# One fused local-attention and mixture-of-experts kernel: the same instructions put in another order by other due times

## The chip, the cores and the metric

The kernel runs on one core of one Trainium2 chip. The metric is the device time of one execution in microseconds (us). The kernel before was timed three times: 1127.76, 1129.4 and 1139.5 us, a median of 1129.4 us. One more execution was profiled; all rows below come from that one.

## The reference, cut to what matters

There are 14336 tokens of width 192. The first half is a dynamic causal convolution: a softmax over 7 generated weights for each token and each of 8 heads, and a weighted sum of the 7 latest rows of `x`.

```python
w = softmax(weight_gen)                       # (B, S, 8 heads, 7 taps)
x = einsum('bshk,bskhg->bshg', w, x_windows)  # 7 shifted rows of x
```

The second half is a noisy top-2 mixture of 8 experts over that result (192 to 1024 to 192, relu):

```python
noisy = x @ w_gate + log1p(exp(x @ w_noise)) * noise
top2 = two largest of noisy;  top2_w = softmax over the two
out[t] = sum over its two e of  top2_w * (relu(x[t] @ w1[e]) @ w2[e])
```

All inputs and the output are fp32. The kernel gets its precision by splitting operands into a high and a low fp16 part and adding the products.

## The kernel before, in words

**Front end.** The tokens are cut into 15 chunks (`COLS`: 4 columns of 128 tokens, then thirteen times 8, then 4). A chunk `c` goes through these stages: loads of `x`, the weights and the noise (`x_loads`, `w_loads`, `n_loads`, issued by SyncE, called SP); sums of squares for a scale (`norms`, ScalarE, L414); the convolution (`conv`, VectorE: 7 products L470 and, from chunk 2 on, 6 sums L501; for chunks 0 and 1 TensorE adds the products up, L486); the split into two halves (`split`, L520 and L528); the gate logits (`gate`: a transpose, on SP as L568 from chunk 2 on, and small products, L575); the routing (`routing`, some 45 small VectorE operations and one small product on TensorE, L715, for the prefix counts); and the scatter (`scatters`, L630: 2 indirect DMAs for each column, issued by GpSimd, called POOL) of each token's record into the queue of its two experts in device memory (`xg`).

**Back end.** The records are taken out in 15 rounds of 8 experts. A block is one expert's 128 rows (round 0) or 256 rows (all others). For a block SP issues transposing loads of its rows (`rows` L1083 and `again` L1088); in front of a round it reads the start of each queue (`entry`), and behind the rows of the round's first block it issues eight loads of the gates' columns (`metas`, L1077). TensorE does the first layer (`mm1`, L1159 and L1165), ScalarE the relu with its high part (`hi`, L1179), VectorE the low part (`lo`, L1183), TensorE the second layer (`mm2`, L1204), ScalarE the gate (`y`, L1216), and POOL adds the rows onto `out` by an indirect DMA (L1221).

**Weights.** Each expert's weights are loaded (`weight_loads`), measured by a Gram product on TensorE (L921), scaled and rounded to a high part on ScalarE (L957, L961, L962), and given a low part: for experts 0 to 3 on TensorE and ScalarE (L998, L999, L1002), for experts 4 to 7 on VectorE (L959, L968, L970).

**What sets the order.** Nothing is ordered on the chip: each engine runs its own list in order, with waits between engines. The lists are written when the program is built, by `Sched`. Each stage is a stream of operations; a step of `Sched` takes, of the operations that could start on an engine within `WAIT` = 0.34 us of the earliest, the one with the earliest due time. The due times come from the two tables that the change touches. `need[b]` is the nominal start of block `b`: `PLAN["start"]` plus the spans of the blocks ahead of it (`SPAN`: 4.4 and 8.2 us); `rounds[c]` is that of a round's first block, `wanted[e]` that of expert `e`'s first block. Each entry of `LEAD` is subtracted from `rounds[c]` ("first" is chunk 0, "second" chunk 1, "last" chunk 14, "rest" the others), each of `PLAN` from `need`, `rounds` or `wanted` (some are added: `finish`, `relu`, `behind`). So a larger lead is an earlier due time. Within one stream nothing changes places: `prologues` gives, for each round, the entries, the rows of the first block, the eight `metas`, and then the rows of the other blocks, whatever their due times are. `SHIFT` moves two blocks of round 0 (experts 6 and 7) in between the blocks of round 1. The durations that `Sched` reckons with, the buffers and the instructions are no part of these tables.

Of the kernel before, what the change touches and what calls it, by code (L numbers as in the profile page):

```python
# [45 lines left out]
PESUM = (0, 1)  # L46
PETR = (0, 1)
LOWPOOL = ()
SHIFT = {6: 4, 7: 2}
YB = 6  # L50
SLOTS = 5
PM0 = 3
PACK = 2
LOWPE = (0, 1, 2, 3)
WAIT = 0.34
PLAN = dict(start=61.4, load=46.6, gram=65.3, high=-15.4, low=13, inverse=19, relu=-7.7, finish=-5, behind=5.2,
            gates=-5.1, entry=-6.7, metas=15.3, rows=10.1, clear=15, zero=18, stray=-10.7, ahead=1, late=2.5,
            landed=1, add=1.5)
SPAN = {256: 8.2, 128: 4.4}
LEAD = {"first": dict(w=112, x=210, n=44, norm=20, conv=23, gap=3.4, split=37, gate=84, route=37, scatter=-13,  # L60
                        every=0),
        "second": dict(w=83, x=31, n=74, norm=115, conv=46, gap=1.4, split=129, gate=49, route=90, scatter=11,
                        every=3.4),
        "rest": dict(w=122, x=117, n=89, norm=107, conv=56, gap=3.7, split=59, gate=36, route=85, scatter=14,
                        every=3.4),
        "last": dict(w=118, x=124, n=45, norm=74, conv=46, gap=1.4, split=72, gate=76, route=51, scatter=15,
                        every=2.8)}
BULK, HEAVY, CLEAN = "SP", "SP", "SP"


# [189 lines left out]
def moe_kernel(ctx, tc, x_lay, wgen, noise, wgn, w1, w2, xg, out):  # L260
# [84 lines left out]
    def bank():  # L345
# [5 lines left out]
    order = sorted(((c, e) for c in range(len(ROUNDS)) for e in range(E)),  # L351
                   key=lambda b: b[0] * E + b[1] if b[0] or not SHIFT.get(b[1]) else E + SHIFT[b[1]] - 0.5 + b[1] / 99)
    need, rounds = [], {}
    t = PLAN["start"]
    for c, e in order:
# [10 lines left out]
    def stages(c):  # L366

        return LEAD["first" if c == 0 else "second" if c == 1 else "last" if c == NC - 1 else "rest"]

# [4 lines left out]
    def before(key, i, n):  # L374

        return [(key, i - n)] if i >= n else []
# [181 lines left out]
    def gate(si):  # L558
# [6 lines left out]
        def transpose(h, t):  # L565
            if t == 0:
                buf[h] = fe.tile([P, 3 * GT, P], F16, name="xtg", bufs=1)
            nc.sync.dma_start_transpose(buf[h][:, 3 * t:3 * t + 3, :], rc[:, a + h + t, 0:RD])  # L568

        def product(h):  # L570
            if not pb:
                pb.append(bank())
            for t in range(GT):
                for b in range(3):
                    nc.tensor.matmul(pb[0][:, (h + t) * 32:(h + t + 1) * 32], buf[h][:, 3 * t + b, :],  # L575
                                     wgu if b == 1 else wga, start=b == 0, stop=b == 2, skip_group_check=True)
# [13 lines left out]
        for h in range(0, n, GT):  # L590
# [8 lines left out]
            for t in range(0 if c in PETR else GT):  # L599
                td = yield ("SP", 1.3, lambda: transpose(h, t), [("loa", si)] + before("gmm", i, 1), 0.6)  # L600
            tp = yield ("PE", 0.12 * GT, lambda: product(h), [td + PLAN["late"] * (c > 1), "wgate"]
                        + (["bank"] + before("bend", c, 2) if h == 0 else []))
# [46 lines left out]
    def routing(c):  # L649
# [67 lines left out]

        to = yield ("PE", 0.35, prefix, [to + PLAN["late"] / 2 * (c > 1), "bank"])
        gg = fs.tile([P, 4, CH], F32, name="gg")
# [35 lines left out]
        for q, (cc, b) in enumerate(ROUNDS):  # L755
# [14 lines left out]
            T["batch", q] = tb  # L770
            sch.spawn(strays(q, t1), PLAN["stray"] - rounds[q])
        if c == NC - 1:
            sch.spawn(count_left(tr), PLAN["stray"] - rounds[len(ROUNDS) - 1])

# [4 lines left out]
    def count_left(t):  # L779

        V = nc.vector

        def add_up():
            with nc.allow_low_precision(reason="counts are exact"):
                V.tensor_reduce(tot, cni, op=OP.add, axis=AX.X)

        t = yield ("DVE", dve(8), lambda: V.tensor_sub(cnt, run, con), [t])
        t = yield ("DVE", dve(8), lambda: V.tensor_scalar(cni, cnt, P - 1.0, None, op0=OP.add), [t])
        t = yield ("DVE", dve(8), lambda: V.tensor_scalar(cni, cni, 7, None, op0=OP.logical_shift_right), [t])
        yield ("DVE", dve(8), add_up, [t])  # L790

    def strays(q, t):

        V = nc.vector
        nt = ROUNDS[q][1] // P
        S = [P, E, nt]
        lim = batches[q][1]
        yield (None, 0.0, None, [t] + before("stray", q, 1))
        m = fs.tile([P, E, NTM], F32, name="mask")[:, :, :nt]

        def out_():
            stray[q] = tabs.tile([P, E, NTM], I32, name="stray")
            V.tensor_mul(stray[q][:, :, :nt], m, none[:, None, :nt].to_broadcast(S))

        d = dve(E * nt)
        t = yield ("DVE", d, lambda: V.tensor_tensor(m, rowi[:, None, :nt].to_broadcast(S),
                                                     lim[:, :, None].to_broadcast(S), op=OP.is_lt), [t])
        T["stray", q] = yield ("DVE", d, out_, [t] + before("round", q, 3))
# [43 lines left out]
    def weight_loads():  # L852
        for e in range(E):
# [12 lines left out]
            ab = [("low1", e - 2)] if e == E - 1 else []  # L866
            ab += before("wab", e, PLAN["ahead"])
            due["load"] = wanted[e] - PLAN["load"]
# [557 lines left out]
```

## Time and profile before

| what | value |
|---|---|
| median of 3 runs (lowest, highest) | 1129.4 us (1127.76, 1139.5) |
| the profiled execution: its time, its span | 1126.05 us, 1124.2 us |
| granted TensorE clock, mean | 0.984 of full speed |
| TensorE busy (matmuls) | 1059.1 us, 94% of the span |
| VectorE busy | 824.0 us, 73% |
| POOL busy | 703.3 us, 63% |
| ScalarE busy | 507.1 us, 45% |

The span runs from the first to the last instruction of the profiled execution; its time holds 1.85 us more. A busy time is the union of an engine's instructions. The rows further down give for each instruction its start and duration in us, and in square brackets the idle time of its engine in front of it and what ended that.

### The profile page before, as it was taken

The numbers are of one execution on the slowest core, as the hardware profiler recorded it, in microseconds if no ns is written. First come the engines' busy times: TensorE is split into PE (matmuls) and PEld (weight loads), VectorE is DVE, ScalarE is ACT, GpSimd is POOL, SyncE is SP. The second block draws the span as 40 slices with busy tenths as digits, with TensorE's granted clock in tenths as the row PEclk, the third lists the DMA queues.
The fourth block names the chain that finished last, engine by engine and source line by source line (L and its number), as shares of the span: only waits on it lengthen the run. The fifth ranks groups of instructions, "written<-read, shape, count | busy, mean of one in ns | idle before, by whom it ended". The sixth has DMA issues, their size and how long they took to land.

```text
span 1124.2 us, 28781 instructions
## 1 busy us (share of the span) xinstructions
PE 1059.1 (94%) x11198; PEld 922.9 (82%) x11198; DVE 824.0 (73%) x1637; ACT 507.1 (45%) x1199; POOL 703.3 (63%) x751
## 2 busy tenths in 40 slices
PE   6988989899899999999999999999999999999995
PEld 3556879889788888898988888788887889898985
DVE  4798889989898979899989898797663533333331
ACT  5578845245345353535435443443333333343432
POOL 0046458788667858788877778667767753434343
PEclk9999989999899999999999999899999999999998
DMA  9979656586788867778587866776654544454322
GB/s 280 284 215 221 131 75 156 75 153 113 118 165 170 141 135 121 163 101 186 87 179 104 169 123 102 155 100 101 106 101 86 95 69 58 57 61 56 53 26 25
DMA packets 274954, 138.19 MB, mean 123 GB/s; under 512 B 207232, under 2 KB 267264, under 8 KB 273152
## 3 DMA queue, kind: packets, MB, share of 16 engines
q1 hardware_dynamic: 230656, 91.02, 38.7%
q0 software_dynamic: 44160, 45.31, 27.3%
q8 instruction: 88, 1.44, 0.5%
q14 instruction: 50, 0.41, 0.1%
HBM read 38.70 MB, written 58.10 MB: 86 GB/s over the span
## 4 chain that ended last, share of the span: by engine, by line
PE 75%; DVE 9%; DMA 5%; issue 4%; ACT 3%; POOL 2%; SPq 2%; another core or an unknown queue 0%; POOLq 0%; DVEq 0%; ACTq 0%
PE py L1204 35%; PE pm L1159 31%; PE pm L1165 5%; DMA out<-y,token 3%; DVE tmp L470 1%; DVE acc L501 1%; POOL out L1221 1%; PE sums L998 1%; DVE lo L1183 1%; ACT junk L414 1%; DVE acc L470 1%; PE py L486 1%; DMA xg<-rec,pos 1%; PE bank L575 1%; SPq L1077 1%
## 5 line engine op out<-in xcount | busy, mean ns | idle before, releaser
L1221 POOL DMA_INDIRECT out<-y,token x232 | 409.3, 1764 | 267.4 <-ACT y L1216 161.8
L1204 PE MATMUL py<-wres,hi 128*128 128x192 f16 x3712 | 478.6, 247 | 4.7 <-issue 4.2
L1183 DVE SCALAR_TENSOR_TENSOR lo<-pm,hi 128x512 f16<-128x512 f32 x464 | 307.6, 686 | 218.5 <-ACT hi L1179 189.8
L1204 PE MATMUL py<-wres,lo 128*128 128x192 f16 x1856 | 458.1, 247 | 9.5 <-DVE lo L1183 7.3
L1159 PE MATMUL pm<-xT,wres 128*128 128x256 f16 (+1 forms) x3968 | 448.9, 271 | 15.4 <-issue 7.3
L1179 ACT ACTIVATE hi<-pm 128x512 f16<-128x512 f32 x464 | 270.2, 596 | 421.0 <-PE pm L1165 191.9
L1159 PEld LDWEIGHTS <-wres 128*128 128x128 f16 x3968 | 376.7, 99 | 63.2 <-issue 20.8
L630 POOL DMA_INDIRECT xg<-rec,pos x224 | 275.0, 1227 | 146.5 <-DVE sm L434 54.5
L1204 PEld LDWEIGHTS <-hi 128*128 128x128 f16 x3712 | 328.6, 98 | 28.5 <-issue 26.1
L1204 PEld LDWEIGHTS <-lo 128*128 128x128 f16 x1856 | 182.1, 98 | 14.0 <-DVE lo L1183 8.4
L470 DVE TENSOR_TENSOR tmp<-xt,wt 128x1536 f32<-128x1536 f32 (+1 forms) x84 | 140.1, 1668 | 3.3 <-PE py L486 2.5
L501 DVE TENSOR_TENSOR acc<-acc,tmp 128x1536 f32<-128x1536 f32 (+1 forms) x78 | 132.0, 1693 | 1.0
L1216 ACT ACTIVATE y<-py,gate 128x192 f32<-128x192 f32 x232 | 89.4, 417 | 67.7 <-PE py L1204 38.3
L623 POOL MEMSET spacer<- 1x1 f32 x272 | 101.7, 374 | 0.1
L1165 PE MATMUL pm<-xT,wres 64*128 64x256 f16 x832 | 65.0, 274 | 0.7 <-issue 0.7
L1165 PEld LDWEIGHTS <-wres 64*128 64x128 f16 x832 | 32.3, 95 | 26.4 <-issue 23.7
L414 ACT ACTIVATE junk<-xt 128x192 f16<-128x192 f32 x118 | 42.4, 359 | 6.3 <-DMA xt<-x_lay 4.3
L470 DVE TENSOR_TENSOR acc<-xt,wt 128x1536 f32<-128x1536 f32 (+1 forms) x21 | 32.9, 1566 | 4.3 <-PE py L486 4.0
L998 PE MATMUL sums<-wres,dg 128*128 128x512 f32 (+1 forms) x64 | 31.3, 572 | 4.6 <-ACT wres L1002 2.4
L528 DVE TENSOR_TENSOR rec<-acc,rec 128x512 f16<-128x512 f32 (+2 forms) x26 | 23.8, 922 | 1.9 <-ACT rec L520 1.1
L520 ACT ACTIVATE rec<-acc 128x1536 f16<-128x1536 f32 (+1 forms) x13 | 18.6, 1431 | 12.8 <-DVE acc L501 12.8
L414 ACT ACTIVATION_READ_ACCUMULATOR junk<-xt 128x1 f32 x118 | 22.4, 190 | 0.0
(155 smaller groups left out, 518.8 us busy)
## 6 DMA issues: line engine op xcount, KB each, us to landing
xt<-x_lay SPq DMA_DIRECT2D x13, 1344.0 KB
out<-zrec SPq DMA_DIRECT2D x13, 768.0 KB
wres<-w SPq DMA_DIRECT2D x6, 768.0 KB
out<-y,token POOLq DMA_INDIRECT x232
xg<-rec,pos POOLq DMA_INDIRECT x224
xT<-xg SPq DMA_TRANSPOSE x224
wres<-w SPq DMA_DIRECT2D x6, 512.0 KB
wres<-w SPq DMA_DIRECT2D x12, 256.0 KB
```

The source lines that it names most:

```text
L414: nc.scalar.activation(q, xtile[s][:, i - first], AF.Square, accum_out=nrm[:, i:i + 1])
L470: V.tensor_mul(tm[key].rearrange("p j (h g) -> p j h g", h=H), xt[:, t:t + n].rearrange("p j (h g) -> p j h g", h=H), w[:, a:a + n].rearra ...
L501: ta = yield ("DVE", cc, lambda: V.tensor_add(tm["acc"], tm["acc"], tm["tmp"]), [tn, ta], None, "two")
L623: nc.gpsimd.memset(spacer, 0.0)
L630: i = nc.gpsimd.indirect_dma_start(out=xg, out_offset=bass.IndirectOffsetOnAxis(ap=idx, axis=0), in_=src, in_offset=None)
L1159: nc.tensor.matmul(dst, w[:, c0:c0 + 128], m, start=k == i == 0, stop=not o.packed and i == 4 and k == o.nf - 1, skip_group_check=True)
L1165: nc.tensor.matmul(dst, w[h, 384:512], x[h], start=False, stop=k == o.nf - 1, skip_group_check=True)
L1179: nc.scalar.activation(h[0][:, :n], pm[:, :n], AF.Relu)
L1183: T["lo", si] = yield ("DVE", dve(n), lambda: nc.vector.scalar_tensor_tensor(h[1][:, :n], pm[:, :n], 0.0, h[0][:, :n], op0=OP.max, op1=OP. ...
L1204: nc.tensor.matmul(dst, h[:, cols], w[:, c0:c0 + D], start=begin, stop=f == F // P - 1 and i == 2, skip_group_check=True)
L1216: nc.scalar.activation(y[0], o.py[t // 2][:, (t % 2) * D:(t % 2 + 1) * D], AF.Copy, scale=gate_of[o.c][:, o.e, t:t + 1])
L1221: i = nc.gpsimd.indirect_dma_start(out=out, out_offset=bass.IndirectOffsetOnAxis(ap=token[o.c][:, o.e, t:t + 1], axis=0), in_=y[0], in_off ...
```

## The change: other due times in three tables

No instruction is added or taken away, and `Sched` itself is the same. `SHIFT` puts the block of round 0, expert 7, behind three blocks of round 1 and no longer behind two. `PLAN` and `LEAD` get other numbers:

```diff
-SHIFT = {6: 4, 7: 2}
+SHIFT = {6: 4, 7: 3}
...
-PLAN = dict(start=61.4, load=46.6, gram=65.3, high=-15.4, low=13, inverse=19, relu=-7.7, finish=-5, behind=5.2,
-            gates=-5.1, entry=-6.7, metas=15.3, rows=10.1, clear=15, zero=18, stray=-10.7, ahead=1, late=2.5,
+PLAN = dict(start=55.4, load=43.9, gram=84.7, high=-36.4, low=12, inverse=21.7, relu=-7, finish=-5.7, behind=5.9,
+            gates=-5.1, entry=-19.7, metas=-20, rows=27.1, clear=15, zero=-3.6, stray=-9.1, ahead=1, late=2.5,
             landed=1, add=1.5)
 SPAN = {256: 8.2, 128: 4.4}
-LEAD = {"first": dict(w=112, x=210, n=44, norm=20, conv=23, gap=3.4, split=37, gate=84, route=37, scatter=-13,
+LEAD = {"first": dict(w=102, x=211, n=42, norm=42, conv=24, gap=2.5, split=36, gate=59, route=13, scatter=13,
                         every=0),
-        "second": dict(w=83, x=31, n=74, norm=115, conv=46, gap=1.4, split=129, gate=49, route=90, scatter=11,
+        "second": dict(w=90, x=39, n=160, norm=102, conv=61, gap=1.4, split=123, gate=51, route=82, scatter=-10,
+                        every=4.2),
+        "rest": dict(w=127, x=97, n=85, norm=126, conv=56, gap=3.7, split=52, gate=36, route=84, scatter=14,
                         every=3.4),
-        "rest": dict(w=122, x=117, n=89, norm=107, conv=56, gap=3.7, split=59, gate=36, route=85, scatter=14,
-                        every=3.4),
-        "last": dict(w=118, x=124, n=45, norm=74, conv=46, gap=1.4, split=72, gate=76, route=51, scatter=15,
-                        every=2.8)}
+        "last": dict(w=139, x=103, n=29, norm=36, conv=27, gap=1, split=92, gate=75, route=30, scatter=20,
+                        every=2.1)}
```

## Rows read from the trace of the kernel before

**Rows 1.** Stretch, its length, busy us of PE PEld DVE ACT POOL, clock, DMA, GB/s.

```profile
0.00:84.00 84.00, 66.02 (x414) 41.33 (x415) 60.55 (x147) 54.18 (x180) 14.00 (x39) 1.00 0.90 261
84.00:224.00 140.00, 127.13 (x1365) 111.87 (x1365) 125.14 (x238) 81.16 (x184) 89.45 (x86) 0.96 0.65 131
224.00:640.00 416.00, 404.72 (x4453) 360.34 (x4452) 378.99 (x715) 187.75 (x453) 318.59 (x307) 0.99 0.77 138
640.00:870.00 230.00, 219.88 (x2347) 191.33 (x2345) 170.39 (x365) 91.17 (x204) 167.97 (x179) 0.98 0.66 114
870.00:1112.00 242.00, 241.35 (x2627) 218.03 (x2624) 88.93 (x174) 92.53 (x181) 110.11 (x138) 1.00 0.44 58
```

**Rows 2.** TensorE's waits, 84 to 224 us: total us, times, longest.

```profile
PE pm L1159 <- DVE lo L1183: 5.8, 2, 3.7
PE py L1204 <- DVE lo L1183: 3.0, 1, 3.0
PE bank L715 <- DVE th L707: 2.1, 1, 2.1
```

**Rows 3.** TensorE's waits, 640 to 870 us.

```profile
PE pm L1159 <- issue: 5.7, 14, 1.2
```

**Rows 4.** The chain that ended last, pieces around the start of round 3.

```profile
283.38 1.22 SPq L1083
...
290.62 3.68 DMA meta<-xg
```

**Rows 5.** Timeline of TensorE: the second layer's wait in round 3.

```profile
298.08 0.34 PE L1204 MATMUL py<-wres,lo 128*128 128x192 f16 x1 [3.15 <-DVE lo L1183]
```

**Rows 6.** Timeline of VectorE, 36 to 57 us: chunk 1's products, the end of chunk 0's routing.

```profile
39.67 1.76 DVE L470 TENSOR_TENSOR tmp<-xt,wt 128x1536 f32<-128x1536 f32 x1 [1.05 <-PE py L486]
...
47.92 1.75 DVE L470 TENSOR_TENSOR acc<-xt,wt 128x1536 f32<-128x1536 f32 x1
49.92 1.75 DVE L470 TENSOR_TENSOR tmp<-xt,wt 128x1536 f32<-128x1536 f32 x1
53.97 0.17 DVE L750 TENSOR_TENSOR rec<-gg,rec 128x4 f32<-128x4 f32 x1
...
54.73 1.75 DVE L470 TENSOR_TENSOR acc<-xt,wt 128x1536 f32<-128x1536 f32 x1
```

**Rows 7.** Timeline of POOL, 57 to 140 us: scatters L630 and adds L1221.

```profile
57.60 1.23 POOL L630 DMA_INDIRECT xg<-rec,pos  x1 [54.54 <-DVE sm L434]
59.13 0.99 POOL L630 DMA_INDIRECT xg<-rec,pos  x1 [0.21 <-issue]
...
62.98 2.07 POOL L630 DMA_INDIRECT xg<-rec,pos  x1 [0.22 <-ACT rec L548]
...
118.40 2.22 POOL L630 DMA_INDIRECT xg<-rec,pos  x1 [0.22 <-issue]
...
127.68 2.28 POOL L1221 DMA_INDIRECT out<-y,token  x1 [2.97 <-ACT wres L961]
```

**Rows 8.** Timeline of SP's queue: the rows of block (1,0).

```profile
124.22 1.22 SPq L1083 DMA_TRANSPOSE xT<-xg  x1
```

**Rows 9.** Timeline of TensorE: the two waits of the first layer in round 1.

```profile
143.55 2.29 PE L1159 MATMUL pm<-xT,wres 128*128 128x256 f16 x10 [3.72 <-DVE lo L1183]
...
153.62 5.14 PE L1159 MATMUL pm<-xT,wres 128*128 128x256 f16 x50 [2.04 <-DVE lo L1183]
```

**Rows 10.** Busy us in one stretch, columns as in Rows 1.

```profile
143.50:147.00 3.50, 3.45 (x19) 2.51 (x19) 3.50 (x5) 2.17 (x3) 0.04 (x1) 0.52 0.29 35
```

**Rows 11.** Timeline of VectorE: low parts of experts 6 and 7.

```profile
144.61 1.81 DVE L959 SCALAR_TENSOR_TENSOR wres<-wc,q,wres 128x1536 f16<-128x1536 f32 x1
...
150.95 1.28 DVE L970 SCALAR_TENSOR_TENSOR wres<-wab,q,wres 128x1024 f16<-128x1024 f32 x1
```

**Rows 12.** Costliest groups on the page: xcount, then busy us, mean ns.

```profile
L414 ACT ACTIVATE junk<-xt 128x192 f16<-128x192 f32 x118 | 42.4, 359 | 6.3 <-DMA xt<-x_lay 4.3
...
L520 ACT ACTIVATE rec<-acc 128x1536 f16<-128x1536 f32 (+1 forms) x13 | 18.6, 1431 | 12.8 <-DVE acc L501 12.8
```

## The prediction, made before the changed kernel was run

> **What bounds the kernel now.** I read the busy times by stretch first, then TensorE's waits, then the chain that ended last, and then the timelines around the places that these name.
>
> The stretches [rows 1] show a kernel held by TensorE from the first block to the last. Its idle time, stretch length less busy time, is 18.0 us up to 84, 12.9 us from 84 to 224, 11.3 us from 224 to 640, 10.1 us from 640 to 870, 0.7 us from 870 to 1112, and 12.2 us from there to the span's end at 1124.2: 65 us in all. An order can't give back more than that, plus what the lower clock costs. The tail comes behind the last matmul and is not touched. In the first 84 us the DMA share is 0.90: loads fill it, and their bytes stay the same. That leaves the 12.9 and the 11.3 us, in which VectorE is busy for 125.1 of 140 and 379.0 of 416 us, as the ones that another order of VectorE's list can move. The 10.1 us are of another kind: there TensorE waits for "issue" [rows 3], nothing that the order names, and VectorE is busy for 170.4 of 230 us only.
>
> In 84 to 224 four waits make 10.9 us [rows 2]: 8.8 us for the low part of a relu and 2.1 us for chunk 1's counts. At the start of round 3 the chain runs scatter, its landing, the rows on SP, the gates' columns, then VectorE [rows 4]; VectorE's list holds the gates' operations ahead of the low parts, and TensorE waits 3.15 us for these [rows 5].
>
> **The change, part by part.** I write r0 for round 0's nominal start; all else counts from it, so `start` itself changes no comparison that I find. Round 1 is at r0 + 26.4, round 2 at r0 + 100.8.
>
> *Chunk 1's convolution against chunk 0's routing.* The routing is due at r0 - 37 before and r0 - 13 after; chunk 1's products are due from r0 - 29.4 before, from r0 - 44.4 after. They change places. Before, the products stand still from 39.67 to 47.92 while the routing runs, and the last begins at 54.73 [rows 6]. A product with its wait for TensorE's sum takes 1.76 + 1.05 = 2.8 us, so without the gap the last would begin at 39.67 + 3 x 2.8 = 48.1: chunk 1 is finished 6.6 us earlier. Three products then run inside the routing where two did, so its end slips by one, 1.75 us, from 54.1 [rows 6]. The first scatter starts at 57.60 [rows 7], 3.5 us behind the routing's end, so it waits for something else as well; whether that covers the slip isn't shown. Bounds: 0 and +1.75; I take **+1.75**, and let it run through the first block's rows to its start.
>
> *What 6.6 us on chunk 1 give.* Its counts come as much earlier, so the 2.1 us wait in TensorE's list [rows 2] goes. What is late next is block (0,0)'s own rows. Bounds 0 and -2.1: **-2.1**.
>
> *Block (0,7) one place later.* The low parts of expert 7's weights were due at r0 + 29.8 and are due at r0 + 39, so they fall behind the low relu parts of block (1,1), due from about r0 + 32. One L959 and two of the L970 kind are 1.81 + 2 x 1.28 = 4.4 us [rows 11], more than the 2.04 us that TensorE waits at 153.62 [rows 9]. The two waits each leave a stretch at the lower clock: behind the first the granted clock is 0.52, that is the 1.2 GHz level [rows 10], and ten matmuls take 2.29 us there against ten out of fifty in 5.14 us further on, 1.03 us [rows 9], so 1.3 us of loss beside the wait. I take the second wait and as much again for its clock as behind the first: **-3.3**. Bounds: 0, if the 4.4 us only move to block (1,2), and -3.3. The first wait (3.72 us) stands behind chunk 2's routing, whose lead changes by one, and stays.
>
> *Weights.* `gram` earlier and `high` 21 us later put a chunk's ScalarE work, one copy of 1.43 us and eight squares of at least 0.36 us [rows 12], some 4.3 us, ahead of the rounding for experts 3 to 5. ScalarE is busy for 54 of 84 and 81 of 140 us [rows 1], so I take **0**; bounds 0 and +4.3. `load`, `zero`, `inverse`, `n`, `w` and `x` change the order on SP only where two loads are ready at once: 0, with bounds of one short wait like that of 2.1 us [rows 2], -2 and +2.
>
> *Rows and gates' columns.* The due times cross over, but both come from one stream, so the eight loads still follow the first rows; entries and columns can only fall behind other loads. **0.** What it would cost if they did is one DMA of them, 3.68 us [rows 4], since VectorE's list waits for them with the low parts behind.
>
> *Chunk 1's scatters.* They are due from r0 - 26.6 to r0 + 36.4 and no longer from r0 - 35.6 to r0 + 15.4, so against the adds of round 0 (due from r0 - 1.3, 4.4 apart) they yield earlier. With the scatters ready 6.6 us earlier, most are out before the first add is: **0**, bounds in the second rival.
>
> *The steady rounds.* For the other chunks `conv`, `gap`, `gate` and `scatter` stay, `route` moves by 1 and `split` by 7; `relu`, `finish` and `behind` move by 0.7 us. At the round starts nothing is loosened [rows 4, 5]. **0**; one wait like that of round 3, 3.15 us, more or less for the range. The last chunk's later stages fall where VectorE is busy for 89 of 242 us [rows 1]: 0.
>
> Sum: +1.75 - 2.1 - 3.3 = -3.7 us. The profiled execution took 1126.05 us, so 1122.4; the median shown is 3.35 us above that execution, and I carry this along: **1125.7**, told as 1126 us.
>
> The trace also shows scatters of 0.99 us and of 2.07 us [rows 7], the long one beside a product of chunk 2's convolution. In the Trainium skill, "SBUF — State Buffer", section "Who interferes with whom", a VectorE instruction with two SBUF inputs contends with a GpSimd instruction that reads SBUF, and the second to issue is blocked. By that rule chunk 2's products, which now begin earlier, would stretch scatters that were short; the third rival prices it from the rows.
>
> **The rivals.** *First, the front end's lead lasts.* If the 6.6 us on chunk 1 reach chunks 2 and 3, the wait of 3.72 us with its 1.3 us of clock, the 3.0 us before round 2 [rows 2, 9] and the 3.15 us of round 3 with as much clock loss [rows 5] go too: 3.7 + 1.3 + 3.0 + 3.2 + 1.3 = 12.5 us more, so 1113 us. For it: VectorE's 90% in both stretches. Against it: the last scatter of a chunk is paced by its due time among the adds, which wait for TensorE, and for chunks 2 and 3 that pacing stays.
>
> *Second, slower: POOL.* If chunk 1's last scatter comes to stand behind the add that starts at 127.68 and takes 2.28 us, it starts at 130 and no longer at 118.40 [rows 7]; round 1's first rows then go out at 136 and not at 124.22 [rows 8]. It decides as soon as TensorE has no other block left, that is with block (0,5) done. The price is 11.6 us, with 1.3 us for the clock 12.9; with no gain of mine kept, 1126.05 + 12.9 + 3.35 = 1142 us. For it: the due times, by which the last four scatters come behind that add, which is block (0,3)'s, and even those of (0,4) and (0,5). Against it: the order takes what is ready, and those adds are ready late.
>
> *Third, scatters under products.* Of chunk 0's eight scatters four are short. Stretched to 2.07 us each they add 4 x 1.08 = 4.3 us ahead of the first rows; instead of my +1.75 that makes 1128 us.
>
> *Fourth, no effect.* Most new due times meet no rival on their engine, and the stalls for "issue" [rows 3] fall elsewhere: 1129 us.
>
> **How the numbers follow.** Forecast 0.45, first rival 0.24, second 0.17, third 0.06, fourth 0.08. The forecast's own range is 1119 to 1135: below, both gains without the slip, one wait of 3.15 us less and the 2 us of SP, 10.5 us under 1129.4; above, the sum with 4.3 us of ScalarE, 2 us of SP and one such wait more, 9.5 us over 1125.7. The 10.1 us of issue stalls may come out several us either way in any case. The range for 8 in 10 takes in most of the first rival and reaches the second: **1109 to 1142**. About 1% is what a measurement can tell here, that is below 1118 or above 1141. Faster: the first rival and little of the forecast, 0.25. Slower: the second rival, and a little for stalls that pile up, 0.19. Within: 0.56.
>
> **What would show it.** Right: chunk 1's products 2.8 us apart without the gap of 8 us; no wait in front of L715 at the first round; the low parts of expert 7 behind those of block (1,1); TensorE's idle time from 84 to 224 at 9 to 11 us and the other stretches as before. Wrong: the idle time from 224 to 640 falls to a few us (first rival); round 1's first rows go out later than 124 us (second); all of chunk 0's scatters are long (third); or the stretch 640 to 870, which I leave alone, moves by more than 5 us.

## The result, and the profile after

| | the kernel before | the changed kernel |
|---|---|---|
| median (lowest to highest), 6 runs each | 1133.13 us (1125.48 to 1141.99) | 1120.93 us (1118.15 to 1123.46) |
| ratio, 95% interval | | 0.9894 [0.9859, 0.9929] |
| profiled execution, span, mean clock | 1126.05 us, 1124.2 us, 0.984 | 1118.29 us, 1116.5 us, 0.988 |

The change makes the kernel about 1.1% faster: 12.2 us between the medians, 7.8 us between the two profiled executions. Run again in another set of runs (r2 below) the ratio was 0.9923 [0.9889, 0.9958]. The forecast was 1126 us. The ratios compare fast executions alone, so they can differ from the quotient of the medians, by up to 0.6% (in e2).

The first view is the table by stretch, with the columns of [rows 1].

```profile
0.00:84.00 84.00, 65.92 (x402) 40.73 (x402) 62.82 (x157) 58.88 (x195) 17.21 (x39) 1.00 0.97 281
84.00:224.00 140.00, 131.79 (x1493) 117.99 (x1493) 130.90 (x248) 79.30 (x176) 99.74 (x93) 1.00 0.67 129
224.00:640.00 416.00, 393.98 (x4315) 350.08 (x4313) 371.08 (x697) 184.87 (x446) 321.99 (x296) 0.98 0.78 139
640.00:870.00 230.00, 222.95 (x2449) 197.39 (x2448) 174.09 (x384) 92.45 (x209) 174.93 (x187) 1.00 0.66 109
870.00:1112.00 242.00, 233.90 (x2548) 211.61 (x2545) 84.13 (x157) 90.39 (x176) 107.97 (x133) 0.99 0.43 56
```

TensorE's idle time is 18.1, 8.2, 22.0, 7.1 and 8.1 us; before [rows 1] it was 18.0, 12.9, 11.3, 10.1 and 0.7 us. From 84 to 224 us 4.7 us are gained, and the clock there is 1.00 where it was 0.96. From 224 to 640 10.7 us are lost again. The last stretch only shows that the work ends earlier.

When the last block of a round gets its gate (the start of the first of its L1216 operations) tells where the lead stands. The last two rows are a second profile of each kernel (r1 and r2 below):

| end of round | 0 | 1 | 2 | 4 | 6 | 7 | 8 | 10 | 14 |
|---|---|---|---|---|---|---|---|---|---|
| before | 191.5 | 227.3 | 294.9 | 436.3 | 571.0 | 639.9 | 707.7 | 857.1 | 1111.6 |
| after | 184.5 | 216.6 | 286.5 | 431.5 | 563.4 | 641.0 | 711.3 | 848.0 | 1103.9 |
| before, r1 | 189.8 | 229.9 | 302.1 | 442.3 | 575.9 | 643.1 | 708.6 | 846.9 | 1102.1 |
| after, r2 | 184.7 | 216.8 | 284.5 | 418.1 | 559.7 | 636.3 | 701.8 | 833.1 | 1088.3 |

The lead is 10.7 us at the end of round 1, 7.6 us at the end of round 6, lost in round 7 (and 3.6 us behind at round 8), back to 9.1 us at round 10 and 7.7 us at the end. In round 7 it is one wait: the first of these views is TensorE's timeline, the second the same place in r2, the third VectorE's timeline in the first run.

```profile
613.80 0.34 PE L1204 MATMUL py<-wres,lo 128*128 128x192 f16 x1 [9.22 <-DVE lo L1183]
```

```profile
609.47 0.34 PE L1204 MATMUL py<-wres,lo 128*128 128x192 f16 x1 [8.44 <-DVE lo L1183]
```

```profile
606.89 0.18 DVE L1124 TENSOR_TENSOR gate<-meta,eid 128x16 f32<-128x16 f32 x1 [7.42 <-DMA meta<-xg]
```

VectorE's list stands 7.42 us at L1124 for the gates' columns, and the low part that TensorE needs is queued behind that, as in round 3 of the kernel before [rows 4, 5].

So the lead of the early rounds is not simply carried to the end. In both pairs of profiles round 7 takes about 9 us of it, and round 9 gives back 7 us: it takes 73.9 and 72.5 us in the kernel before, with 6.83 us at the lower clock (at 720.29 and, in r1, at 744.84), and 66.7 and 65.5 us in the changed kernel, with none. The other rounds differ between the pairs: at the end of round 4 the lead is 4.8 us in the first and 24.2 us in the second.

TensorE's waits from 84 to 224 us, as in [rows 2]:

```profile
PE pm L1159 <- DVE lo L1183: 5.4, 4, 3.3
PE sums L998 <- ACT wres L1002: 2.0, 2, 1.7
PE pm L1159 <- issue: 0.9, 2, 0.4
```

The first layer's waits for low parts are thus 5.4 us where they were 5.8. What is gone is the 3.0 us at L1204, and the wait at L715, which now lies ahead of 84 us (1.74 us, at 81.62). At blocks of 256 rows, where [rows 9] had waits of 3.72 and 2.04 us, there are three short ones, of which one of 0.32 us is not shown; the longest wait, the first line, is at a block of round 0:

```profile
122.57 1.28 PE L1159 MATMUL pm<-xT,wres 128*128 128x128 f16 x20 [3.30 <-DVE lo L1183]
...
138.19 1.25 PE L1159 MATMUL pm<-xT,wres 128*128 128x256 f16 x10 [0.71 <-DVE lo L1183]
...
146.14 2.34 PE L1159 MATMUL pm<-xT,wres 128*128 128x256 f16 x20 [1.03 <-DVE lo L1183]
```

The trace's clock of the kernel before has three stretches of 3.41 us at the 1.2 GHz level in 84 to 224, at 85.4 (behind the wait at L715), 143.4 and 153.7 us. These are windows inside them, in the columns of [rows 1]:

```profile
85.42:88.82 3.40, 3.40 (x24) 2.68 (x24) 3.28 (x9) 2.83 (x7) 0.00 (x0) 0.50 0.75 230
143.45:146.85 3.40, 3.30 (x18) 2.37 (x18) 3.40 (x6) 2.22 (x3) 0.09 (x1) 0.50 0.30 36
153.69:157.09 3.40, 3.40 (x24) 2.75 (x24) 2.88 (x4) 0.09 (x1) 3.08 (x3) 0.50 0.34 49
```

The changed kernel has none there. [Rows 9] price one: ten matmuls in 2.29 us at that level against 1.03 us. At the higher level the work of such a stretch would take about half as long, so one costs about 1.7 us, and three cost 5.1. With the 4.7 us of idle time that is 9.8 of the 10.7 us. This holds for the first pair of profiles alone: in r1 and r2 the clock from 84 to 224 us is 0.96 and 0.97, which makes 1 to 2 us.

The last products of chunk 1 (without the operations between them) and the end of chunk 0's routing, as in [rows 6]:

```profile
38.53 1.76 DVE L470 TENSOR_TENSOR tmp<-xt,wt 128x1536 f32<-128x1536 f32 x1 [1.04 <-PE py L486]
43.32 1.75 DVE L470 TENSOR_TENSOR acc<-xt,wt 128x1536 f32<-128x1536 f32 x1
46.07 1.76 DVE L470 TENSOR_TENSOR tmp<-xt,wt 128x1536 f32<-128x1536 f32 x1
48.65 1.76 DVE L470 TENSOR_TENSOR acc<-xt,wt 128x1536 f32<-128x1536 f32 x1
...
58.03 0.17 DVE L750 TENSOR_TENSOR rec<-gg,rec 128x4 f32<-128x4 f32 x1
```

The gap of 8 us is gone; one of 4.8 us, behind the product at 38.53, is left, with the routing's first operations in it. The last product begins 6.1 us earlier, of which 1.1 us are there already at 38.53, where [rows 6] have 39.67; the routing ends 4.1 us later. POOL's first scatters (without the short operations between them) and SP's rows of blocks (0,0) and (1,0), as in [rows 7, 8]:

```profile
59.13 2.43 POOL L630 DMA_INDIRECT xg<-rec,pos  x1 [56.06 <-ACT jk L925]
61.87 1.21 POOL L630 DMA_INDIRECT xg<-rec,pos  x1 [0.21 <-issue]
63.39 1.47 POOL L630 DMA_INDIRECT xg<-rec,pos  x1 [0.22 <-issue]
65.16 2.18 POOL L630 DMA_INDIRECT xg<-rec,pos  x1 [0.22 <-issue]
```

```profile
80.88 1.32 SPq L1083 DMA_TRANSPOSE xT<-xg  x1
...
124.58 2.17 SPq L1083 DMA_TRANSPOSE xT<-xg  x1
```

The first rows go out 5.1 us later (75.79 before), round 1's at about the same time (124.22 before).

### The profile page after: what moved, and what is told of

Read it like the earlier page. It is cut to its first block, busy times and chain, and to the rows that moved or that the text cites. A ratio compares the mean times of both kernels' runs of the same rounds, so it can differ in the third digit from the quotient of the medians.

```text
span 1116.5 us, 28736 instructions
## 1 busy us (share of the span) xinstructions
PE 1048.5 (94%) x11198; PEld 917.8 (82%) x11198; DVE 823.0 (74%) x1637; ACT 505.9 (45%) x1199; POOL 721.9 (65%) x745
## 4 chain that ended last, share of the span: by engine, by line
PE 78%; DVE 7%; DMA 4%; ACT 3%; issue 3%; SPq 2%; POOL 2%; DVEq 0%; ACTq 0%; POOLq 0%
PE py L1204 36%; PE pm L1159 33%; PE pm L1165 4%; DMA out<-y,token 2%; POOL out L1221 1%; DVE acc L501 1%; DVE tmp L470 1%; ACT junk L414 1%; DVE lo L1183 1%; PE pm L486 1%; DMA xt<-x_lay 1%; PE bank L575 1%; PE sums L998 1%; DMA xg<-rec,pos 1%; PE py L486 1%
## 5 line engine op out<-in xcount | busy, mean ns | idle before, releaser
L1221 POOL DMA_INDIRECT out<-y,token x232 | 413.4, 1782 | 251.5 <-ACT y L1216 147.0
L1204 PE MATMUL py<-wres,hi 128*128 128x192 f16 x3712 | 475.1, 246 | 5.9 <-issue 4.3
L1204 PE MATMUL py<-wres,lo 128*128 128x192 f16 x1856 | 457.0, 246 | 16.3 <-DVE lo L1183 15.4
L1159 PE MATMUL pm<-xT,wres 128*128 128x256 f16 (+1 forms) x3968 | 445.3, 270 | 10.8 <-DVE lo L1183 5.4
L1159 PEld LDWEIGHTS <-wres 128*128 128x128 f16 x3968 | 374.5, 98 | 58.3 <-issue 17.7
L630 POOL DMA_INDIRECT xg<-rec,pos x224 | 289.8, 1294 | 136.2 <-ACT jk L925 56.1
L1204 PEld LDWEIGHTS <-hi 128*128 128x128 f16 x3712 | 327.6, 98 | 26.8 <-issue 25.1
L1204 PEld LDWEIGHTS <-lo 128*128 128x128 f16 x1856 | 181.7, 98 | 19.8 <-DVE lo L1183 16.3
L1216 ACT ACTIVATE y<-py,gate 128x192 f32<-128x192 f32 x232 | 91.4, 418 | 66.9 <-PE py L1204 43.1
L623 POOL MEMSET spacer<- 1x1 f32 x266 | 98.7, 371 | 0.1
L414 ACT ACTIVATE junk<-xt 128x192 f16<-128x192 f32 x118 | 42.5, 360 | 12.4 <-DMA xt<-x_lay 10.3
L998 PE MATMUL sums<-wres,dg 128*128 128x512 f32 (+1 forms) x64 | 30.9, 565 | 4.1 <-ACT wres L1002 3.7
L520 ACT ACTIVATE rec<-acc 128x1536 f16<-128x1536 f32 (+1 forms) x13 | 18.6, 1431 | 17.5 <-DVE acc L501 15.6
```

The source lines that it names most:

```text
L414: nc.scalar.activation(q, xtile[s][:, i - first], AF.Square, accum_out=nrm[:, i:i + 1])
L623: nc.gpsimd.memset(spacer, 0.0)
L630: i = nc.gpsimd.indirect_dma_start(out=xg, out_offset=bass.IndirectOffsetOnAxis(ap=idx, axis=0), in_=src, in_offset=None)
L1159: nc.tensor.matmul(dst, w[:, c0:c0 + 128], m, start=k == i == 0, stop=not o.packed and i == 4 and k == o.nf - 1, skip_group_check=True)
L1204: nc.tensor.matmul(dst, h[:, cols], w[:, c0:c0 + D], start=begin, stop=f == F // P - 1 and i == 2, skip_group_check=True)
L1216: nc.scalar.activation(y[0], o.py[t // 2][:, (t % 2) * D:(t % 2 + 1) * D], AF.Copy, scale=gate_of[o.c][:, o.e, t:t + 1])
```

## The experiments

Four theories were stated. **A**: the gain is made in the first 220 us by the order of chunks 0 and 1 and is carried to the end; the other numbers do nothing. **B**: it is made by the weights' due times in `PLAN`. **C**: any other order moves the loose waits, by chance. **D**: what decides is how long VectorE stands at L1124 for the gates' columns. **E** was formed on what the first ones showed, and is stated with f1 to f3. All ratios are against the kernel before in runs on the same chip; its medians there were 1114.39 us (e1 to e4), 1111.66 us (r1 to e6) and 1131.92 us (f1 to f4).

**One part alone.** On the kernel before:

```diff
e1: LEAD "first" and "second" as in the change
e2: PLAN as in the change
e3: LEAD "rest" and "last" as in the change
e4: -SHIFT = {6: 4, 7: 2}
    +SHIFT = {6: 4, 7: 3}
```

> The kernel before with the new leads of chunks 0 and 1 alone (LEAD first and second). Theory A (the gain is made by the front end's order in the first 220 us and is carried to the end): the last block of round 1 gets its gate 6 to 12 us earlier than at 227.3 us, and the time falls by 6 to 12 us. Rival B (the weights' due times in PLAN make it): within 3 us of before. Rival C (any other order moves the loose waits about by chance): a change of up to 10 us of either sign, made behind 224 us and not ahead of it.

> The kernel before with the new PLAN alone. A: within 4 us of before. B: 6 to 12 us faster, with the last block of round 1 that much earlier. C: up to 10 us of either sign, made behind 224 us.

> The kernel before with the new leads of chunks 2 to 14 alone (LEAD rest and last). A and B: within 4 us of before, since conv, gap, gate and scatter stay and only split and route move. C: up to 10 us of either sign.

> The kernel before with the block of round 0, expert 7, one place later alone (SHIFT). The prediction's own term: 3.3 us faster, the wait of 2.04 us at 153.62 gone and no lower clock behind it. A and B: the same 0 to 3.3 us. C: up to 10 us of either sign.

Measured: e1 1118.3 us, 1.0084 [1.0046, 1.0121]; e2 1119.51 us, 1.0109 [1.0063, 1.0155]; e3 1116.95 us, 1.0045 [0.9999, 1.0091]; e4 1136.59 us, 1.0221 [1.0175, 1.0267]. None is faster, three are slower, and as products they make 1.047 where the whole gives 0.99 (the quotients of the medians, 1.0035, 1.0046, 1.0023 and 1.0199, make 1.03). So neither A nor B stands as put: e1 has A's order and e2 B's. C's 10 us of either sign are 0.9%: e1 and e3 lie within, e2 a little above with an interval that reaches in, e4 outside.

The traces say where it goes. Round 1 ends at 218.7 us in e1, at 214.9 in e3 and at 219.2 in e4, where the kernel before ended it at 227.3 and 229.9 us: three parts make the early gain alone. But round 2 ends at 305.6 us in e1 and 303.3 in e3, against 294.9 and 302.1 us in the two profiles of the kernel before (neither is of the set of e1 to e4). In e4 it ends at 284.5 us, and the lead is lost behind it. Between the ends of rounds 1 and 2 stands, on e1's TensorE:

```profile
229.14 3.15 PE L1159 MATMUL pm<-xT,wres 128*128 128x256 f16 x14 [10.47 <-DMA xT<-xg]
```

The first rows of round 2 are late. Neither the kernel before nor the changed one has such a wait in its first profile.

**The two kernels again, and the gates' columns.** The edit of e5 and e6, on the changed kernel and on the kernel before, makes the planner reckon with gates' columns 6 us later, so that VectorE's list takes other work ahead of them:

```diff
-                                  op=OP.is_equal), [tm])
+                                  op=OP.is_equal), [tm + (6.0 if c > 1 else 0.0)])
```

(L1126 has the same.)

> The kernel before itself, profiled and timed beside the next three, so that all four are read on one chip. Every theory: a ratio of 1.00 within 0.004. Theory D (the round starts decide: VectorE's list stands at the gates' operations until the gates' columns land, and how long differs from run to run and from chip to chip): the total wait of L1124 for the columns differs from the 4.1 us of the first profile by more than 10 us.

> The changed kernel itself, timed beside the kernel before on this chip. A (the gain is made in the first 220 us by the order): a ratio of 0.986 to 0.993 as at first. C and D (the loose waits at the round starts decide): a ratio anywhere from 0.985 to 1.01, and another one than at first.

> The changed kernel, with the planner told that the gates' columns of rounds 2 to 14 land 6 us later than it reckons, so that VectorE's list has low relu parts and products ahead of L1124. D: the wait of L1124 for the columns falls under 5 us in total, and the time falls by 5 to 15 us against the changed kernel. A and C: within 4 us of the changed kernel, or a change without relation to that wait.

> The same edit in the kernel before. D: the wait of L1124 falls under 5 us in total, the time falls by as much as that wait cost TensorE in the kernel before on this chip (0 to 15 us), and ends within 5 us of the changed kernel with the same edit. A: it stays 8 to 12 us behind the changed kernel with the same edit.

Measured: r1 1112.56 us, 1.0016 [0.9981, 1.0051]; r2 1101.73 us, 0.9923 [0.9889, 0.9958]; e5 1129.57 us, 1.0168 [1.0123, 1.0213]; e6 1113.48 us, 1.0056 [1.0022, 1.0091]. VectorE's waits for the columns, here in r1, in r2 and, third, in the first run of the changed kernel (total, times, longest):

```profile
DVE gate L1124 <- DMA meta<-xg: 28.4, 8, 7.9
```

```profile
DVE gate L1124 <- DMA meta<-xg: 24.1, 7, 8.1
```

```profile
DVE gate L1124 <- DMA meta<-xg: 13.5, 5, 7.4
```

In e5 a wait of 10.3 us for the columns is left (D's forecast: under 5 us), and the time is 2.5% above the changed kernel's, where D had 5 to 15 us less. In e6 the whole wait is gone, and the time is not better. D falls as the cause that decides. What the columns alone cost is not priced by these runs, since the edit moved other work too. In e6 TensorE waits for the transposes of a chunk (L568), where r1 has 0.3 us of this:

```profile
PE bank L575 <- DMA xtg<-rec: 9.4, 4, 4.9
```

The wait for the columns also differs much from run to run: the kernel before had 4.1 us of it in its first profile, 28.4 us in r1.

**What makes round 2's rows late: theory E.** It says that the gain needs two things: rounds 0 and 1 without waits, and the next rounds' records scattered in time. In e1 the records are late because of SP's list. Chunk 2's gate logits need eight transposes (L568); this is SP's queue in the changed kernel, and then in e1:

```profile
104.70 4.35 SPq L568 DMA_TRANSPOSE xtg<-rec  x3
109.23 1.19 SPq L1083 DMA_TRANSPOSE xT<-xg  x1
115.08 5.68 SPq L568 DMA_TRANSPOSE xtg<-rec  x4
...
124.58 2.17 SPq L1083 DMA_TRANSPOSE xT<-xg  x1
```

```profile
113.78 1.24 SPq L568 DMA_TRANSPOSE xtg<-rec  x1
115.20 1.18 SPq L1083 DMA_TRANSPOSE xT<-xg  x1
...
124.27 1.28 SPq L1083 DMA_TRANSPOSE xT<-xg  x1
125.77 6.69 SPq L1077 DMA_DIRECT2D meta<-xg  x8
132.66 2.58 SPq L1083 DMA_TRANSPOSE xT<-xg  x2
135.28 4.34 SPq L568 DMA_TRANSPOSE xtg<-rec  x3
```

Three of e1's transposes stand behind a set of weights, round 1's first rows and its eight gates' columns. Chunk 2's routing starts at 145.4 us, ends at 159.1 us (144.9 in the changed kernel), and its sixteen scatters, which POOL takes in turn with the adds, end at 223.3 instead of 197.7 us. e3 has four of them there, the first at 137.78 us. In the kernel before the last four went out at 117.63 us, ahead of the rows at 124.22 [rows 8]. Three experiments put those transposes elsewhere, and one takes the shift out of the whole:

```diff
f1, f2 (on e1, on e3):
-        sch.spawn(gate(si), -lead(c, "gate"))
+        sch.spawn(gate(si), -lead(c, "gate") + 59 * (c == 2))
f3 (on the changed kernel):
-                td = yield ("SP", 1.3, lambda: transpose(h, t), [("loa", si)] + before("gmm", i, 1), 0.6)
+                td = yield ("SP", 1.3, lambda: transpose(h, t), [("loa", si)] + before("gmm", i, 1)
+                            + ([("columns", 1)] if c == 2 and h else []), 0.6)
...
+                T["columns", c] = tm
f4 (on the changed kernel):
-SHIFT = {6: 4, 7: 3}
+SHIFT = {6: 4, 7: 2}
```

> The kernel before with the new leads of chunks 0 and 1 (as in the run e1_chunks01) and, on top, chunk 2's gate stream due 59 us earlier, so that all eight of its transposes (L568) stand on SP ahead of round 1's first rows and its eight loads of gates' columns. In e1 three of them stood behind these, at 135.28 us where the kernel before has them at 117.63, and rows (2,0) came 13.8 us behind the last relu of round 1. Theory E (the early lead is lost because the late transposes make chunk 2's routing and so the rows of round 2 late): chunk 2's routing ends at 144 to 150 and not 159, the stall of 10.5 us at round 2's start goes, round 2 ends at 288 to 296 and not 305.6, and the ratio is 0.985 to 0.998, against 1.008 of e1. Theory A (the gain is made in the first 220 us and carried along whatever follows) can't tell e1 from this one: 1.00 to 1.01. Theory C (waits move by chance): any of 0.99 to 1.02, with a stall at another round start.

> The kernel before with the new leads of the other chunks (as in e3_rest) and chunk 2's gate stream due 59 us earlier; its second four transposes then stand behind one of the eight gates' columns of round 1 and no longer behind all of them, two rows and more. Theory E: routing of chunk 2 ends at 150 to 154 and not 163.6, the 4.4 us stall at 222.8 goes, round 2 ends at 290 to 298 and not 303.3, ratio 0.988 to 1.000 against 1.0045 of e3. Theory A: as e3, 1.000 to 1.009. Theory C: anything between 0.99 and 1.02.

> The changed kernel with one wait more when the order is written: chunk 2's second four transposes come behind round 1's eight loads of gates' columns, as three of them do in e1. Theory E: chunk 2's routing ends at 157 to 160 and not 145, rows (2,0) come 3 to 8 us behind the last relu of round 1 (they were 8 to 11 us ahead of it), a stall of 3 to 8 us stands at the start of round 2, and the ratio goes from 0.992 to 0.997 to 1.005. Theory A: round 1 ends as before at 217, the ratio stays at 0.99 to 0.994. Theory C: no forecast, 0.99 to 1.02.

> The changed kernel with SHIFT as before: block (0,7) behind two blocks of round 1 and no longer three. My prediction priced that move at -3.3 us; on the kernel before alone (e4_shift) it came out at +2.2%. Theory A: the lead at round 1's end is 2 to 4 us smaller (219 to 221), ratio 0.994 to 0.997. Theory E: nothing at the start hangs on it, rows of rounds 2 to 6 in time as in the changed kernel, ratio 0.988 to 0.996. Theory C: 0.99 to 1.02 with a new stall at a round start.

Measured: f1 1149.54 us, 1.0167 [1.0117, 1.0218]; f2 1133.26 us, 1.0022 [0.9982, 1.0063]; f3 1154.75 us, 1.0193 [1.0125, 1.0262]; f4 1118.35 us, 0.9911 [0.9869, 0.9952].

*f3.* The whole change with only these transposes late loses all it gained, and more. On its SP, and on its TensorE at the start of round 2:

```profile
127.55 5.34 SPq L1078 DMA_DIRECT2D meta<-xg  x8
133.08 2.61 SPq L1084 DMA_TRANSPOSE xT<-xg  x2
135.74 3.86 SPq L568 DMA_TRANSPOSE xtg<-rec  x3
```

```profile
223.75 1.46 PE L1161 MATMUL pm<-xT,wres 128*128 128x256 f16 x6 [7.46 <-DMA xT<-xg]
```

Round 1 still ends at 216.3 us. Chunk 2's routing ends at 163.7 us (forecast 157 to 160), the wait is the forecast one (3 to 8 us), and round 2 ends at 297.3 us against 286.5 and 284.5 us in the changed kernel's two profiles. That refutes A: the early gain is there and isn't carried. Theory E forecast a ratio of 0.997 to 1.005 only. The other 20 us are lost later, most in round 4, which takes 95 us (361.2 to 456.1), with chunk 4's routing 25 us later than in the changed kernel; the planner's list behind the edit is another one, and this part was not traced to one place.

*f1.* At round 2 the repair does what E says: transposes at 123.14 us, routing done at 149.3, first rows 12.4 us ahead of the last relu of round 1 and no longer 13.8 us behind it, no wait, round 2 done at 295.8 (forecast 288 to 296). And then the time is worse than e1's, because the same thing happens one chunk on:

```profile
207.91 4.99 SPq L1077 DMA_DIRECT2D meta<-xg  x8
...
223.92 5.10 SPq L568 DMA_TRANSPOSE xtg<-rec  x4
```

```profile
309.76 2.51 PE L1159 MATMUL pm<-xT,wres 128*128 128x256 f16 x11 [15.02 <-DMA xT<-xg]
```

Four transposes of chunk 3 now stand behind round 2's columns and four blocks' rows; in every other kernel here all eight of that chunk are ahead of them. Its routing ends at 247.7 us (213.4 in the changed kernel) and TensorE waits 15.02 us. E's ratio (0.985 to 0.998) was wrong; the mechanism is the one of round 2 in e1. Round 1 ended at 226.7 us in f1, so e1's early gain is not there either; its waits of 3.8 and 3.3 us near 109 us stand at L998, the low parts of weights.

*f2.* The wait of 4.42 us at round 2 falls to none in its profile. Nothing else that E forecast came: chunk 2's routing ends at 157.5 us (forecast 150 to 154), round 2 at 302.1 us (290 to 298; round 1 had ended at 234.3 us already), and the ratio lies above E's range of 0.988 to 1.000, though its interval reaches in, and inside A's.

*f4.* With the old `SHIFT` the whole is as fast as with the new one, as E forecast (0.988 to 0.996). But its round 1 ends at 225.5 us, almost 9 us later than in the changed kernel's two profiles; A had 219 to 221 us, and the early lead that E builds on is not there in this profile.

**All traces side by side.** TensorE's wait for the rows of a round (L1159 for `xT`), one profile each:

| kernel | wait, us | ratio |
|---|---|---|
| changed, twice | 0, 0 | 0.9894, 0.9923 |
| f4 | 0 | 0.9911 |
| before, twice | 0, 7.6 | 1, 1.0016 |
| f2, e3, e6 | 1.6, 4.4, 0 | 1.0022, 1.0045, 1.0056 |
| e1, e2 | 12.1, 10.3 | 1.0084, 1.0109 |
| f1, e5, f3, e4 | 16.8, 15.0, 13.3, 34.7 | 1.0167, 1.0168, 1.0193, 1.0221 |

Every kernel with 10 us or more is slower. What makes the gain is not shown by this: the kernel before had no such wait in its first profile either, and e6 has none and no gain. Nor is it shown that the early rounds decide it: e6 ends round 1 at 224.0 us and f4, in another set, at 225.5, and only f4 is faster (its profiled execution of 1127.39 us was one of its slowest). So late rows of the next round are shown as what takes an early lead away (e1, f3) and as a cost of up to 15 us (f1); what gives the 1% stays open, and C, chance among the loose waits, is not excluded as its source. Open is also this: in e2, e4 and e5 no transposes of chunks 2 to 5 stand behind the columns, so their late rows, e4's longest 13.9 us at 527.8 us, have another cause that was not tested. No version tried beats the changed kernel; f4 is level with it.

## Why the prediction was right, point by point

**The time.** 1120.93 us lies inside the range, and inside the forecast's own range of 1119 to 1135 us. The size of the change does not fit: the sum was -3.7 us, a ratio of 0.997 and outside the measured interval, and 12.2 us were measured between the medians, 7.8 us between the profiled executions. The terms, moreover, were not what made it, so that the time fell inside was luck as far as they go, and owed to the width of the range.

**Chunk 1 against chunk 0's routing.** The swap came in part, with 6.1 us (forecast 6.6), 1.1 us of them from an earlier start and not from the swap, and with 4.8 us of the gap left. The slip was mis-sized, 4.1 us and not 1.75: beside the third product, chunk 2's softmax and scale (L434 to L463, eleven operations of 0.15 to 0.63 us from 51.10 to 57.08 us) had gone into the routing. That it runs through to the end failed: the first rows were 5.1 us late, the first relu 7.7 us, and the end of round 0 was 7.0 us *earlier*. TensorE did other experts' low parts meanwhile: by 91 us 44 of the 64 products of L998 had begun, where it had been 36. I had priced the path of block (0,0) and not asked what TensorE could do in its place. The L715 wait did not go either: it is 1.74 us, now at 81.62, where 2.1 us stood; of that term's -2.1 us 0.4 came.

**Block (0,7).** The term of -3.3 us was mis-sized and misplaced. The wait of 2.04 us at 153.62 went, but so did most of the 3.72 us [rows 9], which I had held fixed because chunk 2's routing lead "changes by one"; chunk 2's routing ended 5.6 us earlier all the same, and chunk 1's 4.0 us. A wait of 3.30 us at a block of round 0 took their place. The sign came by half: of expert 7's three low parts one (L959, at 140.33 us) still ran ahead of block (1,1)'s, and two, at 147.20 and 148.39 us, behind the first two of these. And f4 shows that the move is worth nothing measurable in the whole, e4 that alone it costs 2.2%.

**The clock.** I counted 1.3 us for one stretch at the lower level; three went, about 5.1 us. In the first pair of profiles this term carried as much of the early lead as the waits; in the second it is 1 to 2 us.

**SP and the gates' columns.** I took 0 because "both come from one stream". Within the stream the order holds, but another stream crosses it: expert 6's weights went out at 66.88 us, ahead of the first rows, where they had been at 84.67, behind. And the crossing of chunk 2's transposes with round 1's columns, which I had not listed at all, is what f3 prices at 7.46 us at round 2 alone.

**The steady rounds** were not "as before": 10.7 us were lost from 224 to 640, 9.2 of them in the wait at 613.80, and 3.0 us gained from 640 to 870 (forecast: within 5).

**The rivals.** The first (the lead lasts, 1113 us) was half right: the lead of 10.7 us was about as large as its 12.5, and about 8 us stood at the end. But its sign did not come, since the idle time from 224 to 640 rose to 22.0 us and did not fall to a few. The second, POOL, did not come: round 1's rows went out at 124.58 us, not 136. The third's mechanism came, its price did not. Chunk 0's eight scatters take 14.1 us where they took 10.9; the first, at 59.13, lay under chunk 2's first two products and took 2.43 us, and with the later start the first rows were late. Over all 224 scatters of the changed kernel the median is 0.98 us for those beside no product or sum of a convolution and 1.66 us for those with over 0.5 us beside one. This agrees with the Trainium skill, "SBUF — State Buffer", section "Who interferes with whom": a VectorE instruction with two SBUF inputs contends with a GpSimd instruction that reads SBUF. The longer scatters cost nothing at the end of round 0, for the reason given under the first point. The fourth, no effect, is out by the interval.

## What to carry to other kernels

In a kernel whose lists are written by a planner, a due time isn't a local edit: four parts that gained nothing or cost up to 2.2% alone made 1% of gain together, so price an order as a whole and look at the release of each next round, not only at the stage that was moved. Follow each chunk's chain from the first transfer that shares a queue with another stream; here three or four transposes behind eight small loads went with waits of 4 to 15 us at the start of the next round. A first block that starts later cost nothing here, where the bound engine had other work. A short wait can cost more than its length: the three of 2.1, 3.7 and 2.0 us in the kernel before [rows 2, 9] had a stretch at the lower clock behind them, while the changed kernel's 3.30 us at 122.57 had none (in r2, 2.26 us at the same place had one).

## What the runs showed of the hardware

The same kernel before took 1133.13, 1114.39, 1111.66 and 1131.92 us in four sets of runs, a level that moved more than the change; only ratios within one set could be used. TensorE's waits that the rows put down to "issue" [rows 3] go with that level. Over the whole span they come to 12.0 to 18.7 us in the six profiles of the first and the last set (the two kernels, f1 to f4), and the eight profiles of the two faster sets (e1 to e6, r1, r2) show none. The levels lie 17.5 to 21.5 us apart, so these waits may be most of it. What they are stays open. This is the stretch from 640 to 870 us in r2, columns as in [rows 1], where the changed kernel had 7.1 us of idle time in its first profile:

```profile
640.00:870.00 230.00, 230.00 (x2571) 207.81 (x2566) 179.29 (x405) 97.42 (x203) 182.11 (x199) 1.00 0.71 112
```
